# Transposes in halves, and another order of all instructions, in a long-convolution and MLP kernel

## The chip, the cores and the metric

The kernel runs on one core of one Trainium2 chip. The metric is the device time of one launch in microseconds (us), lower is better. A core has a matrix engine (TensorE, PE in the profile), VectorE (DVE), ScalarE (ACT), GpSimd (POOL) and SyncE (SP), each with an instruction list of its own that it works off strictly in order; 16 DMA engines move data for the queues of SP and POOL. Engines meet through semaphores: an instruction whose operand isn't ready waits, and everything behind it on its engine waits too.

## What is computed

One gated layer with two branches on 2048 rows of 640 columns, all in bf16:

```python
def _A_ref(q, k, v, shift_k, ssm_k, ssm_D):          # long convolution
    k_pad = jnp.pad(k, ((0, 0), (ks - 1, 0), (0, 0)))
    for t in range(ks):                              # ks = 4 taps along the rows
        k_shift = k_shift + k_pad[:, t:t + S, :] * shift_k[:, ks - 1 - t]
    kv = k_shift * v
    y = irfft(rfft(kv, 2 * S) * rfft(ssm_k, 2 * S))[:S]   # each column by itself
    return q * (y + kv * ssm_D)
def _B_ref(x, w1, w2, w3, w4):                       # MLP
    h = _gelu(_layernorm(x) @ w1)
    # the four quarters of h are moved by 1, -1, 2, -2 rows
    x1 = x + shifted(h) @ w2
    return x1 + _gelu(_layernorm(x1) @ w3) @ w4
g = _sigmoid((A_q * gate_w).sum(-1))
return g * _A_ref(A_q, ...) + (1 - g) * _B_ref(A_q, ...)
```

The column counts are 640 for the branches' inputs and outputs and 1536 for the inner width of the second MLP (w3, w4).

## The kernel before

**Recording, then emitting.** Small helpers (`tt` and `ts` for VectorE, `act` for ScalarE, `mm` for TensorE, `P.dma` for the queues) don't issue anything: each records an operation with what it reads and writes, in the order of the code. There are 1196 operations. `Prog.schedule` (line 255) then puts them into the order of one list, `SEQUENCE` (line 457), whose entries are indices of recording; `Prog.emit` (276) gives each engine its own operations in that order and adds the waits that the data needs. A second list, `PLACES` (522), gives each of the 205 accumulation tiles its bank of PSUM; an operation that opens a tile waits until the users of the bank's former tile are through. So the order of every engine, of SyncE's and POOL's DMA queues too, is one list written out by hand. As the helpers issue everything, the profile names their lines: L616 a VectorE operation on two tensors, L621 one with scalars, L626 ScalarE, L636 TensorE, L235 a transposing DMA, L238 any other DMA, L900 the residual of mm2.

**The convolution.** The 640 columns are five chunks c of 128, the 2048 rows four blocks of 512; the convolution is done block by block with a folded Fourier transform written as matrix products. A chunk passes these stages:
- `h_load` (712) loads 128 rows of the filter; `h_fold` (715) makes the sums and differences that a real transform of half the size needs, the four sums first (`sd[:, 0]`) and then the four differences (`sd[:, 1]`), and one DMA transposes all 2048 columns so that `h_chunk` (745) can take the spectrum HF on TensorE.
- `kv_load` (750) brings a chunk of keys and one of values from HBM through a transposing DMA each (2048 rows by 128 columns, 512 KB). Keys go to one of two buffers in turn (`kT[c % 2]`). `kv_taps` (757) makes the four shifted multiples of the keys on VectorE (four 2048-wide operations of L621, "taps"), adds them and multiplies by the values.
- `kv_fold` (777) is the same fold for that product, again with one transposing DMA at its end, and `x_chunk` (789) takes the spectrum XF. Chunks 1 to 4 use the same memory (`kv_at`, 559): the first tap of chunk c + 1 writes where the transpose of kv_fold-c reads, and its third tap where that transpose writes and x_chunk-c reads.
- `combine` (949) adds neighbouring blocks of XF. `unit` (955) multiplies spectra (2560-wide products of L616, and accumulating DMAs on POOL's queue for part of the sums). The buffers of the last units lie over those of the late folds.
- `final` (994) takes a unit back by matrix products with G, multiplies by q and adds to the output: the first 12 by an accumulating DMA on POOL's queue, whose VectorE buffer `gyb[k % 8]` is used again eight steps later, the last four by a plain write from SyncE.

**The MLP** works by row tiles t (16 of 128 rows) and row groups (four of 512). `ln1` (833) normalizes (the first half of the tiles is transposed on TensorE, the later ones by DMA), `mm1` (851) and `mmg` do the first product and the shifts, `mm2` (886) the second with the residual, `ln2` (906) normalizes again: its *apply* (L621, 640 wide) writes one of two buffers `xn2[t % 2]`, and a transposing DMA of 160 KB takes it into `xT`. So the apply of ln2-3 waits until the transpose of ln2-1 has read its buffer. `mm3` (917) and `mm4` (938) are the second MLP, `base` (933) writes the first part of the output rows, mm4 adds to it by an accumulating DMA on POOL's queue.

**SyncE's list** starts with 22 plain loads, then all transposes and later loads follow. In operations by name ("T" for a transpose, "k" and "v" for the keys and values of kv_load):

```
x_load-0 (2), x_load-1, x_load-0 (2), x_load-1, w1 (2), h_load-1, w2, h_load-0, x_load-3, x_load-2,
cR, w3 part 0, w2 (2), x_load-2, w2 (2), x_load-3, cRh,
kv_load-1 k T, kv_load-1 v T, kv_load-0 v T, h_fold-0 T, kv_load-0 k T, ln1-8 T, ln1-9 T, h_fold-1 T, ...
kv_load-4 k T, base-4, kv_load-3 v T, kv_fold-2 T, ln2-9 T, base-8, base-9, cG, ln2-8 T, w4, kv_load-4 v T, ...
```

cR and cRh are the constants of the forward transforms, w1 to w4 the weights.

Of the kernel before, what the change touches and what calls it, by code (L numbers as in the profile page):

```python
# [420 lines left out]
def bass_gated_mix__ssm_conv_h3__mixer_s_mlp__prompt_kernel(  # L421
# [4 lines left out]
    P = Prog(nc)  # L426
# [26 lines left out]
    def ps(n, cls):  # L453
# [3 lines left out]
    SEQUENCE = [27, 10, 47, 6, 0, 11, 29, 4, 9, 1, 3, 46, 2, 30, 5, 12, 8, 7, 26, 13, 131, 14, 49, 15, 48, 16, 28, 54, 17, 132,  # L457
# [257 lines left out]
    def h_fold(c):  # L715
# [11 lines left out]
        tt(sd[:, 1], pm[:, :, :, 0:128], rev, ALU.subtract)  # L727
        tt(sd[:, 0, 0, :, 0], pm[:, 0, :, 128], rev[:, 0, :, 0], ALU.add)
        ts(sd[:, 0, 1, :, 0], pm[:, 1, :, 128], 1.0, None, ALU.mult)
        P.dma(sp, ft, V(h_at[c], 2048), transpose=True)  # L730

    def spectrum(c, f, F_, even, odd):
        for j in range(4):
# [402 lines left out]
```

## Time and profile before

| | us |
|---|---|
| median of the runs (three) | 246.19 |
| lowest and highest of them | 245.36 and 246.31 |
| the profiled execution | 244.31 |
| its span, from the first to the last instruction | 242.5 |
| TensorE busy in the span | 217.8 (90%) |
| VectorE busy | 218.5 (90%) |
| ScalarE busy | 171.2 (71%) |
| POOL busy | 66.5 (27%) |

The profile is one execution, seen by the hardware profiler. An engine's busy time is the time of its instructions; the rest of the span it waits, for another engine or for a DMA, or for its own queue. Rows of the timeline give the start in us from the span's start, the length, the engine, the line, the operation with what it writes and reads, the count, and in brackets the idle time of the engine just ahead of it with what ended it. `arena` is the one large buffer in which nearly all data lie, so the names of buffers say little; which stage an instruction belongs to follows from its place in its engine's list. In a row of the groups, the time behind the bar is the busy time and the mean of one in ns, then the idle time ahead with its releasers. The queue's own rows (SPq) give what an issue occupied on SyncE.

### The profile page before, as it was taken

Reading aid. Unit: us, or ns where it says so; the run is one execution under the profiler, and the core shown is the slowest. Engines: PE = TensorE matmul, PEld = TensorE weight load, DVE = VectorE, ACT = ScalarE, POOL = GpSimd, SP = SyncE. Lnnn points to the kernel's source line nnn. Section 1 sums busy time; section 2 is a strip of 40 time slices with the busy share of each in tenths; the row PEclk is TensorE's granted clock in tenths of the full one; section 3 lists DMA queues with packets and bytes.
Section 4 is the critical chain, followed back from the end, with each engine's and each line's share of the span. In section 5 each row is a group of like instructions: output and inputs, shape, how many; then the busy total and the mean of one; then the engine's idle time right before and its main releaser. Section 6 shows DMA issues by size and latency. Waiting matters only on the chain.

```text
span 242.5 us, 3885 instructions
## 1 busy us (share of the span) xinstructions
PE 217.8 (90%) x1428; PEld 126.5 (52%) x1428; DVE 218.5 (90%) x431; ACT 171.2 (71%) x307; POOL 66.5 (27%) x70
## 2 busy tenths in 40 slices
PE   7889899898899987998889989999999999998950
PEld 2677675354344445345465437764576545775520
DVE  5999999999599868899599699999999999999974
ACT  2598569995689959997799766256876455246951
POOL 1311135402000011103342401431115203557591
PEclk9999999999999999999999999999999999999985
DMA  6999999999999998998918955399998914999998
GB/s 185 341 381 330 155 209 171 224 230 190 225 197 204 247 121 182 224 329 185 172 32 164 186 90 162 32 150 200 187 255 132 164 22 73 175 172 172 119 111 160
DMA packets 79970, 44.02 MB, mean 182 GB/s; under 512 B 59337, under 2 KB 75214, under 8 KB 79950
## 3 DMA queue, kind: packets, MB, share of 16 engines
q1 hardware_dynamic: 70944, 31.89, 56.1%
q0 software_dynamic: 8832, 11.80, 33.3%
q8 instruction: 11, 0.18, 0.3%
q10 hardware_dynamic: 174, 0.07, 0.1%
q14 instruction: 9, 0.07, 0.1%
HBM read 14.92 MB, written 6.55 MB: 89 GB/s over the span
## 4 chain that ended last, share of the span: by engine, by line
DVE 56%; DMA 20%; ACT 9%; issue 6%; PE 4%; POOL 2%; SPq 2%; POOLq 0%; DVEq 0%
DVE arena L616 45%; DMA arena<-arena 13%; ACT arena L626 9%; DVE arena L621 6%; PE PSall L636 4%; DMA out_dram<-arena 4%; DMA arena<-in_A_ssm_k_dram 3%; DVE arena L798 3%; DVE arena L865 2%; SPq L238 2%; POOL out_dram L238 1%; POOL arena L238 0%; DVE arena L799 0%; DVE arena L900 0%; DVE arena L682 0%
## 5 line engine op out<-in xcount | busy, mean ns | idle before, releaser
L636 PE MATMUL PSall<-arena 128*128 128x320 bf16 (+4 forms) x1367 | 209.4, 310 | 17.5 <-ACT arena L626 6.6
L636 PEld LDWEIGHTS PSall<-arena 128*128 128x128 bf16 x1367 | 122.0, 98 | 104.1 <-ACT arena L626 17.2
L616 DVE TENSOR_TENSOR arena<-arena 128x2560 bf16<-128x2560 bf16 (+9 forms) x217 | 162.6, 807 | 6.0 <-DMA arena<-arena 2.5
L626 ACT ACTIVATE arena<-PSall 128x512 bf16<-128x512 f32 (+7 forms) x169 | 102.3, 652 | 30.0 <-PE PSall L636 24.8
L626 ACT ACTIVATE arena<-arena 128x640 bf16<-128x640 bf16 (+6 forms) x72 | 49.1, 705 | 15.7 <-DVE arena L616 11.3
L802 POOL TENSOR_TENSOR arena<-arena 128x1 f32<-128x1 f32 (+1 forms) x26 | 23.1, 919 | 98.6 <-DVE arena L621 98.6
L621 DVE TENSOR_SCALAR arena<-arena 128x1 f32<-128x1 f32 (+5 forms) x110 | 33.5, 339 | 10.6 <-DMA arena<-arena 5.8
L238 POOL DMA_DIRECT2D out_dram<-arena x28 | 29.4, 1320 | 44.6 <-ACT arena L626 39.1
L626 ACT ACTIVATE arena<-PSall,arena 128x640 bf16<-128x640 f32 (+1 forms) x32 | 20.7, 653 | 18.9 <-PE PSall L636 18.8
L238 POOL DMA_DIRECT2D arena<-arena x12 | 14.5, 1205 | 27.4 <-DVE arena L616 25.2
L798 DVE BATCH_NORM_STATS2 arena<-arena 128x6 f32<-128x320 bf16 x32 | 14.3, 481 | 1.7 <-DMA arena<-in_A_q_dram 1.6
L662 PE MATMUL PSall<-arena 128*128 128x512 bf16 x15 | 5.8, 570 | 1.6 <-DVE arena L658 1.6
L900 DVE SCALAR_TENSOR_TENSOR arena<-PSall,arena 128x640 bf16<-128x640 f32 x8 | 6.5, 817 | 0.7 <-PE PSall L636 0.7
L865 DVE TENSOR_SCALAR arena<-arena 32x256 bf16<-32x256 bf16 (+1 forms) x24 | 5.8, 242 | 0.4
L626 ACT ACTIVATE PSall<-PSall 128x640 f32<-128x640 f32 x8 | 5.5, 692 | 0.1
L662 PEld LDWEIGHTS PSall<-arena 128*128 128x128 bf16 x15 | 2.0, 139 | 4.9 <-issue 3.0
L844 PE MATMUL PSall<-arena 128*128 128x128 bf16 x40 | 3.5, 220 | 0.6 <-DVE arena L621 0.5
L844 PEld LDWEIGHTS PSall<-arena 128*128 128x128 bf16 x40 | 2.4, 98 | 1.3 <-DVE arena L621 1.1
L665 ACT ACT_TABLE_LOAD x1 | 1.3, 1283 | 2.1 <-issue 2.1
L799 DVE BATCH_NORM_AGGREGATE arena<-arena 128x2 f32<-128x12 f32 x16 | 2.6, 190 | 0.0
L626 ACT ACTIVATION_READ_ACCUMULATOR arena<-arena 128x1 f32 x8 | 1.8, 221 | 0.0
L626 ACT ACTIVATION_READ_ACCUMULATOR arena<-PSall 128x1 f32 x8 | 1.6, 194 | 0.0
(21 smaller groups left out, 5.6 us busy)
## 6 DMA issues: line engine op xcount, KB each, us to landing
arena<-arena POOLq DMA_DIRECT2D x12, 640.0 KB, 6.7
arena<-in_A_q_dram SPq DMA_DIRECT2D x14, 320.0 KB, 6.2
out_dram<-arena POOLq DMA_DIRECT2D x20, 160.0 KB, 5.4
arena<-in_A_ssm_k_dram SPq DMA_DIRECT2D x5, 512.0 KB, 4.5
arena<-in_B_w_dram SPq DMA_DIRECT2D x1, 1920.0 KB, 9.1
out_dram<-arena SPq DMA_DIRECT2D x10, 160.0 KB, 2.3
arena<-in_B_w_dram SPq DMA_DIRECT2D x1, 1152.0 KB, 11.9
out_dram<-arena SPq DMA_DIRECT2D x12, 80.0 KB, 3.0
```

Of the source, the lines that this page charges most:

```text
L238: fn = lambda e: e.dma_start(out, in_, **kw)
L616: P.op(eng, lambda e: e.tensor_tensor(o, real(a), real(b), op), [a, b], [o], dve_ns(o, [a, b], 2) if eng == "dve" else 500)
L621: P.op(eng, lambda e: e.tensor_scalar(o, real(a), s1, s2, op0=op0, **({} if op1 is None else {"op1": op1})), [a] + aps, [o], n_of(o) / 3.8 ...
L626: P.op("act", lambda e: e.activation(real(o), real(a), f, bias=bias, scale=scale, **({"accum_out": accum} if accum is not None else {})), ...
L636: fns.append(lambda e, l=l, r=r, i=i: e.matmul(real(o), l, r, start=(i == 0), stop=(i == last)))
L662: P.op("pe", lambda e: e.matmul(real(pw), warm[:, 0:128], warm[:, 128:640], start=True, stop=True), [warm], [pw], 427.0 if i < 14 else 216.0)
L798: P.op("dve", lambda e, o=o, i=i: e.bn_stats(o, i), [i], [o], 400)
L799: P.op("dve", lambda e: e.bn_aggr(bna[:, t, :], bns[k]), [bns[k]], [bna[:, t, :]], 120)
L802: P.op("pool", lambda g: g.tensor_tensor(o, a, e, ALU.pow), [a, e], [o], dur)
L844: P.op("pe", [lambda e, c=c, pb=pb, xn=xn: e.transpose(real(pb)[:, 128 * c:128 * (c + 1)], xn[:, 128 * c:128 * (c + 1)], ident) for c in r ...
L865: P.op("dve", lambda e, o=hT[q, 4, c0:c0 + n], i=hx[q, :]: e.tensor_scalar(o, i, 1.0, None, op0=ALU.mult), [hx[q, :]], [hT[q, 4, c0:c0 + n ...
L900: P.op("dve", lambda e: e.scalar_tensor_tensor(x, real(pr), 1.0, x, op0=ALU.mult, op1=ALU.add, accum_out=st[1, 0][:, t:t + 1]), [pr, x], [ ...
```

## The change

The transposes of `h_fold`, `kv_load` and `kv_fold` (20 in all) are issued as two each: for keys and values the first and the second 1024 rows, for the folds the sums and the differences. Every other operation is recorded as before.

```diff
@@ h_fold
-        P.dma(sp, ft, V(h_at[c], 2048), transpose=True)
+        for i in range(2):
+            P.dma(sp, ft[:, 8 * i:8 * i + 8, :], V(h_at[c] + 1024 * i, 1024), transpose=True)
@@ kv_load
-        P.dma(sp, kT[c % 2][:, 16:2064].unsqueeze(1), A_k[0, :, cs], transpose=True)
-        P.dma(sp, V(kv_at[c], 2048).unsqueeze(1), A_v[0, :, cs], transpose=True)
+        for i in range(2):
+            P.dma(sp, kT[c % 2][:, 16 + 1024 * i:1040 + 1024 * i].unsqueeze(1), A_k[0, 1024 * i:1024 * i + 1024, cs], transpose=True)
+        for i in range(2):
+            P.dma(sp, V(kv_at[c] + 1024 * i, 1024).unsqueeze(1), A_v[0, 1024 * i:1024 * i + 1024, cs], transpose=True)
@@ kv_fold
-        P.dma(sp, V(kv_at[c] + 6144, 2048).rearrange("p (q c) -> p q c", q=16), V(kv_at[c] + 2048, 2048), transpose=True)
+        for i in range(2):
+            P.dma(sp, V(kv_at[c] + 6144 + 1024 * i, 1024).rearrange("p (q c) -> p q c", q=8), V(kv_at[c] + 2048 + 1024 * i, 1024), transpose=True)
```

`SEQUENCE` and `PLACES` are replaced as a whole (1216 operations, again 205 tiles):

```diff
-    SEQUENCE = [27, 10, 47, 6, 0, 11, 29, 4, 9, 1, 3, 46, 2, 30, 5, 12, 8, 7, 26, 13, 131, 14, 49, 15, 48, 16, 28, 54, 17, 132,
...
+    SEQUENCE = [27, 10, 46, 8, 1, 30, 11, 5, 9, 4, 0, 48, 3, 29, 2, 12, 28, 13, 47, 26, 14, 33, 15, 49, 16, 50, 17, 34, 51, 41,
...
-    PLACES = [0, 0, 2, 3, 1, 3, 7, 4, 1, 6, 7, 0, 4, 4, 2, 4, 2, 4, 0, 3, 2, 7, 0, 4, 1, 5, 7, 6, 2, 6, 7, 2, 1, 4, 4, 1, 0,
...
+    PLACES = [7, 2, 6, 0, 4, 2, 2, 3, 6, 6, 5, 6, 4, 2, 6, 0, 2, 5, 0, 5, 4, 5, 3, 0, 1, 7, 3, 1, 1, 0, 7, 1, 0, 7, 3, 1, 2,
...
```

By name, the places of the new order that matter below (a and b are the first and second half of a transpose):

```
SyncE, start: x_load-0 (3), w1, x_load-0, w1, x_load-1 (2), x_load-2, w2, h_load-0, w2 (4), x_load-2, x_load-3 (2),
  kv_load-1 k b, kv_load-0 k a, kv_load-0 k b, h_load-1, cRh, h_fold-0 a, h_fold-0 b, kv_load-0 v b, kv_load-1 k a,
  ln1-8 T, ln1-9 T, h_load-2, ...; w3 part 0 behind h_fold-2 a, cR behind kv_fold-1 a
SyncE, around ln2-3: kv_fold-0 b, a, ln2-0 T, ln2-1 T, kv_fold-1 b, h_fold-4 b, a, kv_fold-1 a, cR, ln2-3 T, ln2-2 T
SyncE, around kv_fold-2: kv_load-4 k b, kv_load-3 v b, ln2-7 T, kv_load-3 v a, kv_fold-2 b, a, ln2-6 T, w4, base-1, ln2-9 T
VectorE, from the last fold result to the buffer's next use:
  kv_fold-2 to kv_taps-3   before: three residuals of mm2, a tap, small ones; after: a tap, an apply of ln2, small ones
  kv_fold-3 to kv_taps-4   before: a tap, a combine, small ones; after: four combines, a tap, small ones
  kv_fold-4 to unit-0-3    before: two products, a small one; after: two products, a combine, small ones
TensorE, behind the start of x_chunk-2: before 7 groups of mm3-0 after its end; after 3, the others ahead of it
POOL, end, before: mm4-13, final-0-3-0, -0-1-0, -0-2-1, mm4-14, final-0-0-1, -0-0-0, -0-3-1, -0-1-1, final-1-...
POOL, end, after: mm4-15, mm4-14, final-0-1-1, -0-0-1, mm4-13, final-0-3-0, -0-2-0, -0-1-0, -0-3-1, -0-0-0, final-1-...
```

139 rows, old and new, of tables (PLACES, SEQUENCE) are left out of this document.

## The prediction

> **What bounds the kernel now.** The stretches come first: busy time of each engine, then granted clock, DMA share and GB/s.
>
> ```profile
> core 0: us, PE busy (x) PEld busy (x) DVE busy (x) ACT busy (x) POOL busy (x), PEclk, DMA share, GB/s
> 0.00:15.00 15.00, 11.99 (x121) 7.44 (x121) 11.80 (x49) 7.36 (x21) 3.28 (x9) 1.00 0.87 285
> 15.00:60.00 45.00, 40.21 (x338) 26.07 (x337) 43.96 (x133) 35.76 (x76) 10.83 (x12) 1.00 1.09 228
> 60.00:140.00 80.00, 73.61 (x397) 37.30 (x395) 65.81 (x129) 69.76 (x112) 14.87 (x15) 1.00 0.90 190
> 140.00:222.00 82.00, 81.06 (x512) 49.53 (x509) 81.73 (x82) 46.15 (x77) 25.82 (x26) 1.00 0.77 141
> 222.00:239.20 17.20, 10.98 (x67) 6.13 (x66) 15.20 (x44) 12.13 (x25) 11.69 (x10) 0.88 1.08 130
> ```
>
> From 140 to 222 TensorE (81.06 of 82) and VectorE (81.73 of 82) are both full, so nothing can be won there. VectorE is idle for 14.2 us between 60 and 140 and for 1.0 us between 15 and 60; TensorE is idle for 6.4 and 4.8 us there. The change removes no arithmetic. The run therefore gets shorter only by idle time that **both** engines lose before 140, or in the tail. Who ends that idle time is read from the waits between 60 and 140 (total, times, longest), then from single rows of the timeline.
>
> ```profile
> DVE arena L621 <- DMA arena<-arena: 5.3, 3, 2.8
> DVE arena L621 <- ACT arena L626: 3.9, 4, 2.8
> DVE arena L616 <- DMA arena<-arena: 2.2, 1, 2.2
> ACT arena L626 <- DMA arena<-arena: 4.0, 2, 2.5
> ```
>
> ```profile
> 65.56 0.45 DVE L621 TENSOR_SCALAR arena<-arena 128x640 bf16<-128x640 bf16 x1 [2.76 <-DMA arena<-arena]
> 90.59 0.74 ACT L626 ACTIVATE arena<-arena 128x640 bf16<-128x640 bf16 x1 [2.52 <-DMA arena<-arena]
> 91.45 0.21 DVE L621 TENSOR_SCALAR arena<-arena 128x1 f32<-128x1 f32 x1 [2.77 <-ACT arena L626]
> 117.67 0.75 DVE L621 TENSOR_SCALAR arena<-arena 128x2048 bf16<-128x2048 bf16 x1 [1.79 <-DMA arena<-arena]
> 120.09 0.74 ACT L626 ACTIVATE arena<-arena 128x640 bf16<-128x640 bf16 x1 [1.45 <-DMA arena<-arena]
> 135.31 1.49 DVE L616 TENSOR_TENSOR arena<-arena 128x2560 bf16<-128x2560 bf16 x1 [2.24 <-DMA arena<-arena]
> ```
>
> The reader is to see that every DMA named here goes from the arena to the arena on SyncE's queue: a transpose. By their place in VectorE's list the stalls are: 65.56, the apply of ln2-3, whose buffer xn2 the transpose of ln2-1 still reads; 91.45, ln2-8, behind the ScalarE square of mm2-8, which waits for the transpose of ln2-6; 117.67, the first tap of chunk 4, whose buffer the transpose of kv_fold-3 still reads; 135.31, the first product of unit-0-3 that goes into a buffer under kv_fold-4. The third wait of the first row (5.3 - 2.76 - 1.79, so 0.77) is the same for kv_fold-2 and chunk 3. TensorE stalls on the same thing:
>
> ```profile
> 44.42 12.55 PE L636 MATMUL PSall<-arena 128*128 128x512 bf16 x83 [1.06 <-DMA arena<-arena]
> 58.09 2.58 PE L636 MATMUL PSall<-arena 128*128 128x1 bf16 x20 [1.12 <-DMA arena<-arena]
> 61.67 9.79 PE L636 MATMUL PSall<-arena 128*128 128x512 bf16 x48 [1.00 <-DMA arena<-arena]
> 92.44 17.63 PE L636 MATMUL PSall<-arena 128*128 128x320 bf16 x89 [2.31 <-ACT arena L626]
> 121.88 18.38 PE L636 MATMUL PSall<-arena 128*128 128x320 bf16 x102 [1.43 <-ACT arena L626]
> ```
>
> The last two follow the ScalarE stalls at 90.59 and 120.09, so all five are late transposes: 6.9 us. **Late transposes are the bound of the stretch before 140.** Why they are late, SyncE's queue and the landings tell:
>
> ```profile
> 17.08 9.04 SPq L235 DMA_TRANSPOSE arena<-in_A_k_dram  x1
> 31.66 2.42 SPq L235 DMA_TRANSPOSE arena<-arena  x1
> 60.90 1.28 SPq L235 DMA_TRANSPOSE arena<-arena  x1
> L235 SPq DMA_TRANSPOSE arena<-arena x34: 1199/1278/3608, 31.7 to 148.0; - x34
> L235 SPq DMA_TRANSPOSE arena<-in_A_k_dram x5: 2286/3050/9036, 17.1 to 87.5; - x5
> L235 SPq DMA_TRANSPOSE arena<-in_A_v_dram x5: 1428/2133/2710, 26.2 to 108.3; - x5
> arena<-in_A_v_dram SPq DMA_TRANSPOSE x1, 4.1
> arena<-arena SPq DMA_TRANSPOSE x1, 2.6
> ```
>
> Rows of line 235 give issue time on SyncE (least, median, most, in ns); the last two are the landings of kv_load-4's value transpose at 108.35 (512 KB, 4.1 us) and of ln2-14's at 147.99 (160 KB, 2.6 us), both with little beside them. The first transpose holds SyncE until 26.1, while the plain loads before it drain.
>
> **The change, part by part.** *SyncE's start.* The old list puts 7.3 MB of plain loads ahead of the first transpose, the new one some 2.5 MB less (the 1152 KB of w3, 512 KB of h_load-1, cR's 384 and cRh's 480 KB go behind). At the 285 GB/s of the first row that is 9.1 us by which the first transposes can start earlier; h_fold-0's, issued at 31.66, stands in the new list directly behind what VectorE needs to make it. Nobody needs the loads that move back at once: w3 and cR are first used in stages after 75 us. h_load-1 and cRh are needed earlier, by VectorE's h_fold-1 and TensorE's h_chunk-0 near 25 to 30 us; both now stand behind three key halves on SyncE, at 1.2 to 2.13 us each 3.6 to 6.4 us, less than the 9.1 won. If that cover is gone, each us that they are late costs one us of both engines there. *Halves.* A 160 KB transpose takes 1.2 us of SyncE at the least, a 512 KB one 1.4 to 3.6, so two halves cost 2.4 against a middle of 2.6 (medians 2.13 and 3.05). The trace has no 256 KB transpose; between the rows above it lands in 2.6 + 1.5 x 96/352 = 3.0 us. From 1.2 us a half (2.4 a pair) to 2.13 (4.3 a pair), I take 1.3, nearest to the many small ones: 12 pairs stand before ln2-2 in the new list, and cost nothing as long as the lead of 9.1 us covers them. I charge 0.5 us for what shows.
>
> *VectorE's order around the folds.* For this I count the work that stands between the last instruction that feeds a transpose and the first that needs its buffer, at busy time over count of these groups:
>
> ```profile
> L616 DVE TENSOR_TENSOR arena<-arena 128x2560 bf16<-128x2560 bf16 x52 | 74.7, 1480 | 2.3 <-DMA arena<-arena 2.2
> L616 DVE TENSOR_TENSOR arena<-arena 128x1024 bf16<-128x1024 bf16 x40 | 26.1, 683 | 0.2
> L616 DVE TENSOR_TENSOR arena<-arena 128x1280 bf16<-128x1280 bf16 x28 | 22.2, 814 | 0.3 <-DMA arena<-arena 0.3
> L621 DVE TENSOR_SCALAR arena<-arena 128x2048 bf16<-128x2048 bf16 x20 | 14.8, 745 | 3.4 <-DMA arena<-arena 2.6 <-PE PSall L636 0.8
> L900 DVE SCALAR_TENSOR_TENSOR arena<-PSall,arena 128x640 bf16<-128x640 f32 x8 | 6.5, 817 | 0.7 <-PE PSall L636 0.7
> L636 PE MATMUL PSall<-arena 128*128 128x512 bf16 x430 | 97.1, 379 | 3.3 <-DMA arena<-arena 2.1 <-ACT arena L626 0.5 <-DVE arena L621 0.3
> ```
>
> That is 1.44 us for a unit product, 0.65 for a fold half, 0.79 for a combine, 0.74 for a tap, 0.82 for a mm2 residual; the smallest I take at 0.15.
> - kv_fold-4 to unit-0-3: before 2 products and a small one, 3.0; after 2 products, a combine and four small, 4.3. The stall of 2.24 shrinks by 1.3, and by up to 0.65 more because the first half leaves after one fold subtraction or sum and not after both. I take -1.9 (from -1.3 to -2.2).
> - kv_fold-3 to chunk 4: before a tap, a combine and three small, 2.0; after four combines, a tap and three small, 4.4. All of the 1.79 goes: -1.8.
> - kv_fold-2 to chunk 3: before three residuals, a tap and six small, 4.1; after a tap, one 640-wide apply and four small, 1.8. **This one gets worse by 2.3.** Its half b is queued first and waits for the later of the two fold results, so the split wins nothing here. Behind this tap in VectorE's list stand all taps of chunk 3, and ln2-9 and ln2-8.
> - ln2-3: about as much work between (6.8 after, 6.4 before), but ln2-1's transpose now stands behind kv_fold-0's and not behind a key transpose of 512 KB; ln2-6: its transpose is now queued behind both halves of kv_fold-2. Each wins between 0 and 2.77; the trace can't say more, I take half: -1.4 each.
>
> Sum for VectorE: -1.9 - 1.8 + 2.3 - 1.4 - 1.4 = -4.2.
>
> *TensorE's order.* It must win as much. In the old list h_chunk-2 follows h_fold-2 so closely that TensorE has 3.8 us more work ahead of it than VectorE has ahead of the fold; in the new one this is over 6 for every transpose that TensorE uses, against 4.1 to 5 us for issue and landing. I count two thirds of the 6.9 us as gone, 4.6, which covers VectorE's 4.2. One wait is added: the third tap of chunk 3 overwrites what x_chunk-2 reads, and in the new list four more groups of mm3-0 (20 matmuls at 0.226, 4.5 us) stand before the end of x_chunk-2; with 0.7 less VectorE work before the tap the wait tightens by 5.2. 2.3 of it are the kv_fold-2 stall already counted, the other 2.9 are covered if TensorE has won 2.9 by then; four of its five stalls (5.5 us) lie before that place, two thirds are 3.7. So nothing, and 2.9 if not. *PSUM banks*: new places alter who waits for whose eviction; TensorE's waits for ScalarE beside the two above are small, so 0, within 1 us either way.
>
> *Tail.* POOL's last accumulating writes free VectorE's gy buffers:
>
> ```profile
> 229.51 6.17 POOL L238 DMA_DIRECT2D out_dram<-arena  x5 [2.35 <-DVE arena L616]
> 233.39 3.62 DVE L616 TENSOR_TENSOR arena<-arena 128x320 bf16<-128x320 bf16 x14 [1.55 <-DMA out_dram<-arena]
> ```
>
> The write of final-0-3-1-1 moves ahead of two others on POOL's queue, but VectorE has 5.2 instead of 6.1 us of work until it reuses that buffer: 0, from -1.6 to +1.
>
> **Sum:** -4.2 + 0.5 = -3.7 us. The profiled execution (span 242.5) took 244.31 us, 1.9 less than the median of the three runs, 246.19. 244.31 - 3.7 = 240.6; the same difference from the median gives 242.5.
>
> The Trainium skill, "DMA: Bandwidth & Descriptors", section "Rules for kernel authors", speaks against the split: two transfers to disjoint halves use the same 16 engines and serialize, so one should be used. The landings of 4.1 and 2.6 us agree with a part that doesn't scale. By that rule the 0.65 us of the early half go, and the sum is about -3.1: 243.1.
>
> **Rivals.** *Forecast*, 240 to 245: chance 0.52. *More*: all five TensorE stalls go, and VectorE's waits at best (-2.2, -1.8, -2.8, -2.8, tail -1.6, +2.3 for kv_fold-2, so -8.9) are capped by TensorE's 6.9: 239.3. For it speaks that both engines are full afterwards; against it, that the chain from kv_fold-2 gets longer, and that TensorE's ScalarE waits at 92.44 and 121.88 go only if both ln2 transposes come earlier. 0.16. *Traded*: TensorE doesn't get ahead, and the 2.9 us at x_chunk-2 stand: -3.7 + 2.9 = -0.8, 245.4. For it speaks that DMA is at 1.09 between 15 and 60 whatever the order. 0.14. *Slower*: the queue. Place: SyncE, from the first transpose to ln2-2. If a half takes as long as what a whole value transpose takes in backlog, the 24 halves push everything behind them. It decides from (9.1/12 + 2.6)/2 = 1.7 us a half, where the lead is used up; at 1.9 it is 24 x 0.19 = 4.6 us late on both engines: 250.8. For it: SyncE issues without a pause from 17 to 75; against it: the median of 1.28. 0.18. The same section's rule to coalesce small transfers would favour this case.
>
> **Numbers.** 0.5% of 246.19 is 1.2 us, about what a measurement can tell from no change. Forecast and *more* are faster, 0.68; *traded* is the same, 0.14; *slower* 0.18. The range leaves out the lower end of *more* and the upper of *slower*: 237.5 to 248.5; the forecast's own is 240 to 245.
>
> **What would show it.** Right: the first transpose issued before 17 and finished before 20; VectorE idle under 10.5 between 60 and 140; the waits at chunk 4 and unit-0-3 under 0.7 each, that at chunk 3 near 3; TensorE's waits for DMA arena<-arena under 1.1. Wrong: a median issue of halves above 1.7 us, VectorE waiting over 4 us for TensorE at chunk 3, or a tail after TensorE's full stretch longer than 17 us.

## The result, and the profile after

| | us |
|---|---|
| kernel before, median of 20 runs | 245.9 (243.41 to 247.66) |
| changed kernel, median of 20 runs | 247.55 (245.83 to 250.44) |
| ratio, 95% interval | 1.008 (1.0051 to 1.0109) |
| profiled execution of the changed kernel, its span | 246.26, 244.5 |

The change makes the kernel 0.8% slower, where 1.5% faster was forecast: about 2 us lost instead of 3.7 won. The ratio leaves out the slowest executions (one of the changed kernel, two of the one before), so it is not quite that of the two medians. The stretches of the changed kernel, in the columns of before:

```profile
core 0: us, PE busy (x) PEld busy (x) DVE busy (x) ACT busy (x) POOL busy (x), PEclk, DMA share, GB/s
0.00:15.00 15.00, 12.72 (x150) 8.70 (x151) 11.99 (x49) 7.99 (x23) 3.55 (x9) 1.00 0.91 285
15.00:60.00 45.00, 40.90 (x301) 25.03 (x303) 43.46 (x117) 35.97 (x76) 6.00 (x6) 1.00 1.05 204
60.00:140.00 80.00, 71.76 (x406) 37.49 (x412) 68.37 (x142) 62.49 (x99) 16.60 (x16) 1.00 0.89 180
140.00:222.00 82.00, 75.14 (x465) 46.19 (x468) 75.09 (x77) 48.17 (x83) 37.77 (x28) 0.96 0.84 160
222.00:244.00 22.00, 15.01 (x100) 8.90 (x97) 19.29 (x49) 13.87 (x27) 14.66 (x13) 0.92 1.10 139
```

From 60 to 140 VectorE is idle for 11.6 us instead of 14.2: something was won there. But from 140 to 222, where both engines had been full, each is now idle for 6.9 us. What they wait for, from the waits of that stretch (total, times, longest):

```profile
PE PSall L637 <- ACT arena L627: 6.6, 1, 6.6
DVE arena L617 <- DMA arena<-arena: 6.0, 1, 6.0
```

It is one event. (The changed kernel's lines stand one to five further down than those of before: L617 is its L616, L622 its L621, L807 the power on POOL that was L802. The kernels of experiments 3, 5, 8, 9 and 10 have the line numbers of before.) The chain that ended last, in order of time, runs through it; the columns are start, length and what:

```profile
153.70 0.14 DVE arena L622
153.84 0.07 issue
153.91 10.19 POOL arena L807
164.09 7.56 DMA arena<-arena
171.75 3.64 DVE arena L617 x3
```

By their places in the lists: at 153.70 VectorE makes the variance of ln2-14. POOL raises it to the power -1/2, an operation on 128x1 elements that for the other tiles of ln2 took between 0.5 us (0.55 for ln2-11) and 2.5 us (2.46 for ln2-13) in this execution and lasts 10.2 us here. Behind it on POOL's queue stands the second accumulating DMA of unit-0-2, whose last operand VectorE had finished at about 156. It is issued at 164.09 and lands at 171.66. VectorE needs the sum and stops for 6.02 us; ScalarE's next copy waits for VectorE and TensorE for ScalarE. During the power VectorE runs eight two-tensor operations back to back, and the power ends 0.4 us after the last of them:

```profile
153.74 9.97 DVE L617 TENSOR_TENSOR arena<-arena 128x1280 bf16<-128x1280 bf16 x8
153.91 10.22 POOL L807 TENSOR_TENSOR arena<-arena 128x1 f32<-128x1 f32 x1 [0.58 <-DVE arena L622]
```

In the kernel before, the power of ln2-14 ran at 134.0, in VectorE's wait for kv_fold-4, and took 1.05 us:

```profile
134.00 1.05 POOL L802 TENSOR_TENSOR arena<-arena 128x1 f32<-128x1 f32 x1
```

TensorE's stop is followed by a lower granted clock, 0.57 between 172 and 180, which is the 0.96 of the stretch; VectorE is busy without a pause there, so no further loss is seen from it.

The waits of VectorE between 60 and 140, from the waits and the timeline:

```profile
DVE arena L622 <- DMA arena<-arena: 6.6, 3, 4.6
DVE arena L617 <- issue: 1.9, 1, 1.9
```

```profile
88.34 1.23 DVE L617 TENSOR_TENSOR arena<-arena 128x2048 bf16<-128x2048 bf16 x1 [1.86 <-issue]
90.49 0.45 DVE L622 TENSOR_SCALAR arena<-arena 128x640 bf16<-128x640 bf16 x1 [0.93 <-DMA arena<-arena]
100.55 0.75 DVE L622 TENSOR_SCALAR arena<-arena 128x2048 bf16<-128x2048 bf16 x1 [4.58 <-DMA arena<-arena]
116.70 0.75 DVE L622 TENSOR_SCALAR arena<-arena 128x2048 bf16<-128x2048 bf16 x1 [1.05 <-DMA arena<-arena]
```

Gone are the waits at ln2-3 (2.76), ln2-8 (2.77), unit-0-3 (2.24) and in the tail (1.55). The tap behind kv_fold-2 waits 4.58 instead of 0.77, that behind kv_fold-3 1.05 instead of 1.79. New are 1.86 at chunk 2's product with its values (their second half landed at 88.26) and 0.93 at ln2-7. Together -9.32 + 3.81 - 0.74 + 1.86 + 0.93 = -3.46 us. With the 6.02 us behind POOL that is +2.6, and the spans differ by +2.0; the rest are small waits and 0.3 us less busy time.

SyncE's issues say why kv_fold-2 got worse by more than the 2.3 foreseen:

```profile
89.02 2.64 SPq L235 DMA_TRANSPOSE arena<-in_A_k_dram  x2
91.71 1.28 SPq L235 DMA_TRANSPOSE arena<-in_A_v_dram  x1
93.04 1.27 SPq L235 DMA_TRANSPOSE arena<-arena  x1
94.36 1.30 SPq L235 DMA_TRANSPOSE arena<-in_A_v_dram  x1
95.70 4.35 SPq L235 DMA_TRANSPOSE arena<-arena  x3
L235 SPq DMA_TRANSPOSE arena<-in_A_k_dram x10: 1287/1300/4510, 10.1 to 107.4; - x10
L235 SPq DMA_TRANSPOSE arena<-in_A_v_dram x10: 1233/1300/1333, 27.3 to 115.6; - x10
arena<-arena SPq DMA_TRANSPOSE x3, 3.5
```

The fold was done at about 94.6. Its two halves were issued at 95.70 and 97.05, behind four halves of keys and values and a transpose of ln2, each 1.3 us on SyncE. A half takes as long to issue as the short ones of before and lands in 3.5 us (the last row, the median of the two halves and the 160 KB transpose that follows), where 3.0 was estimated.

### The profile page after: what moved, and what is told of

Same layout as the page of the kernel before. It is cut to its first block, busy times and chain, and to the rows that moved or that the text cites. A ratio compares the mean times of both kernels' runs of the same rounds, so it can differ in the third digit from the quotient of the medians.

```text
span 244.5 us, 3915 instructions
## 1 busy us (share of the span) xinstructions
PE 215.5 (88%) x1413; PEld 126.3 (52%) x1428; DVE 218.2 (89%) x431; ACT 168.5 (69%) x307; POOL 78.6 (32%) x70
## 4 chain that ended last, share of the span: by engine, by line
DVE 38%; PE 21%; DMA 19%; POOL 7%; SPq 5%; issue 5%; ACT 2%; DVEq 0%; POOLq 0%
DVE arena L617 26%; PE PSall L637 21%; DMA arena<-arena 11%; DVE arena L622 6%; POOL arena L807 5%; SPq L235 5%; DVE arena L803 4%; DMA arena<-in_A_v_dram 3%; POOL out_dram L238 2%; DMA arena<-in_A_ssm_k_dram 2%; DMA out_dram<-arena 2%; DMA arena<-in_A_q_dram 2%; ACT arena L627 2%; DVE arena L870 1%; SPq L238 1%
## 5 line engine op out<-in xcount | busy, mean ns | idle before, releaser
L637 PE MATMUL PSall<-arena 128*128 128x320 bf16 (+4 forms) x1352 | 208.3, 311 | 20.6 <-ACT arena L627 11.6
L617 DVE TENSOR_TENSOR arena<-arena 128x2560 bf16<-128x2560 bf16 (+7 forms) x217 | 163.6, 810 | 10.8 <-DMA arena<-arena 6.0
L627 ACT ACTIVATE arena<-PSall 128x512 bf16<-128x512 f32 (+6 forms) x169 | 100.8, 647 | 41.7 <-PE PSall L637 37.4
L807 POOL TENSOR_TENSOR arena<-arena 128x1 f32<-128x1 f32 (+1 forms) x26 | 35.1, 1374 | 108.6 <-DVE arena L622 108.5
L627 ACT ACTIVATE arena<-arena 128x640 bf16<-128x640 bf16 (+6 forms) x72 | 48.2, 697 | 17.5 <-DVE arena L617 14.3
L622 DVE TENSOR_SCALAR arena<-arena 128x1 f32<-128x1 f32 (+5 forms) x110 | 33.5, 339 | 7.1 <-DMA arena<-arena 6.7
L238 POOL DMA_DIRECT2D out_dram<-arena x28 | 32.0, 1492 | 12.3 <-ACT arena L627 10.6
L238 POOL DMA_DIRECT2D arena<-arena x12 | 16.7, 1434 | 39.3 <-DVE arena L617 39.3
L627 ACT ACTIVATE arena<-PSall,arena 128x640 bf16<-128x640 f32 (+1 forms) x32 | 20.1, 658 | 9.4 <-PE PSall L637 9.1
L627 ACT ACTIVATION_READ_ACCUMULATOR PSall<-PSall 128x1 f32 x8 | 1.6, 197 | 0.0
```

The lines of the kernel that those rows point to most:

```text
L238: fn = lambda e: e.dma_start(out, in_, **kw)
L617: P.op(eng, lambda e: e.tensor_tensor(o, real(a), real(b), op), [a, b], [o], dve_ns(o, [a, b], 2) if eng == "dve" else 500)
L622: P.op(eng, lambda e: e.tensor_scalar(o, real(a), s1, s2, op0=op0, **({} if op1 is None else {"op1": op1})), [a] + aps, [o], n_of(o) / 3.8 ...
L627: P.op("act", lambda e: e.activation(real(o), real(a), f, bias=bias, scale=scale, **({"accum_out": accum} if accum is not None else {})), ...
L637: fns.append(lambda e, l=l, r=r, i=i: e.matmul(real(o), l, r, start=(i == 0), stop=(i == last)))
L807: P.op("pool", lambda g: g.tensor_tensor(o, a, e, ALU.pow), [a, e], [o], dur)
```

## The experiments

Lists below name instructions in the order of one engine; everything else is as in the kernel named. Each ratio is to the kernel before on the same chip.

**1. The power behind the DMA.** Theory: the wait is a queue, and the power has no turn while VectorE is busy. On POOL, in the changed order:

```diff
-  mm4-5, power of ln2-14, unit-0-2 second DMA, mm4-4
+  mm4-5, unit-0-2 second DMA, power of ln2-14, mm4-4
```

> The changed kernel with one instruction moved: on POOL, the small operation of ln2-14 (L807, 128x1) stands behind the second accumulating DMA of unit-0-2, not ahead of it. In the changed kernel that operation lasted 10.22 us (153.91 to 164.13, while VectorE ran eight two-tensor products without a pause), the DMA behind it was issued at 164.09 though its data were ready at about 156, and VectorE waited 6.02 us for its landing at 171.66. Theory (the queue): the DMA is issued near 156, lands before 165, VectorE's wait of 6.02 is under 0.5, and the time falls by 5 to 6.5 us, to 241 to 242.5, below the kernel before. The POOL operation still lasts until VectorE pauses. Rival (slow DMA): the DMA lands late anyway, because POOL cannot issue while VectorE runs or because the 16 engines are taken; VectorE still waits 4 us or more there and the time is within 1 us of 247.5. Rival (elsewhere): the wait goes but another takes its place further on; 245 to 247.5.

Measured 241.15 us, ratio 0.9841 (0.9789 to 0.9893): by the ratios 2.4% or 5.9 us under the changed kernel, and faster than before. POOL's part of the timeline:

```profile
158.24 1.20 POOL L238 DMA_DIRECT2D arena<-arena  x1 [2.92 <-DVE arena L617]
158.98 7.14 POOL L807 TENSOR_TENSOR arena<-arena 128x1 f32<-128x1 f32 x1
```

The DMA is issued while VectorE is busy, in the usual 1.20 us, as soon as its operand is there (this execution ran 2 us later than the one above), and lands at 164.09, 3.5 us before VectorE needs it. The power still lasts 7.14 us, until VectorE pauses for its result. So the place behind the power in POOL's queue is what cost the time, and neither POOL's issuing nor the DMA engines.

**2. A pause for the power.** The rival to test is that the power is slow by itself. POOL's list is left as it is; on VectorE the instruction of ln2-14 that needs the power moves up:

```diff
-  unit-0-2 product 3, six operations, ln2-14 (waits for POOL)
+  unit-0-2 product 3, ln2-14 (waits for POOL), six operations
```

> The changed kernel with one instruction moved: on VectorE, the small operation of ln2-14 that waits for POOL's result stands directly behind the product that ends at 155.96 (unit-0-2, product 3) instead of six instructions later, so VectorE pauses there. POOL's list is that of the changed kernel. Theory (POOL's operation gets no turn while VectorE runs two-tensor operations back to back): it ends some 0.4 us after VectorE has paused, so it lasts 2.3 to 2.8 us instead of 10.2; VectorE waits about 0.5 us for it, the wait of 6.02 goes, the time is 241 to 243. Rival (the operation is slow by itself at this place, for instance because POOL has first to fetch something): it still lasts about 10 us, VectorE waits about 8 us for it, and the time is 246.5 or more.

Measured 240.3 us, ratio 0.9822 (0.9777 to 0.9866).

```profile
154.45 2.47 POOL L807 TENSOR_TENSOR arena<-arena 128x1 f32<-128x1 f32 x1 [0.58 <-DVE arena L622]
156.89 1.20 POOL L238 DMA_DIRECT2D arena<-arena  x1
156.96 0.16 DVE L617 TENSOR_TENSOR arena<-arena 128x1 f32<-128x1 f32 x1 [0.46 <-POOL arena L807]
```

VectorE gives up 0.46 us and the power takes 2.47 us instead of 10.22. The rival falls: what the power lacks is a turn.

**3. The new order with whole transposes.**

```diff
@@ kv_fold; h_fold and kv_load likewise, each at the place of its later half
-        for i in range(2):
-            P.dma(sp, V(kv_at[c] + 6144 + 1024 * i, 1024).rearrange("p (q c) -> p q c", q=8), V(kv_at[c] + 2048 + 1024 * i, 1024), transpose=True)
+        P.dma(sp, V(kv_at[c] + 6144, 2048).rearrange("p (q c) -> p q c", q=16), V(kv_at[c] + 2048, 2048), transpose=True)
```

> The new order of everything with whole transposes: each pair of halves is one transpose of 512 KB at the place of the later half. It tells what the halves are worth in the new order. By the prediction's step they cost 0.5 us of queue and win 0.65 us at unit-0-3, so nothing: 246.5 to 248.5, with the same 6 us wait behind POOL. Rival (halves burden SyncE's queue or the DMA engines): the time falls by 2 us or more, below 245.5. Rival (halves are what the new order rests on): over 249.5, with waits of VectorE for transposes in the stretch from 60 to 140 grown by 2 us or more.

Measured 246.59 us, ratio 1.004 (1.0004 to 1.0076). The wait behind POOL is there as before:

```profile
152.58 10.22 POOL L802 TENSOR_TENSOR arena<-arena 128x1 f32<-128x1 f32 x1 [0.58 <-DVE arena L621]
170.43 1.49 DVE L616 TENSOR_TENSOR arena<-arena 128x2560 bf16<-128x2560 bf16 x1 [6.04 <-DMA arena<-arena]
```

Against the changed kernel's 1.008 the halves would cost about 1 us, but the two intervals overlap, so this alone does not show it. Both rivals fall: the time is neither 2 us lower nor 3 us higher.

**4. The old order with halves**, the two of a pair directly behind each other.

> The old order of everything, with each of the 20 whole transposes issued as two halves directly behind each other. It tells the price of the halves alone. By the prediction's row (2.4 us for a pair against a middle of 2.1 for a whole) the queue before 60 us grows by some 4 us for 12 pairs and, without the earlier start, part of it shows: 246.5 to 249.5. Rival (a half costs as much as a whole on the queue): over 250. Rival (the early half wins everywhere): under 245.

Measured 248.83 us, ratio 1.0141 (1.0085 to 1.0198): 3.5 us for the halves alone where the order wasn't made for them. So they are not free there; what the new order is worth without them, the next experiment tells.

**5. Whole transposes and the pause**, experiments 2 and 3 together.

> The new order with whole transposes, and the VectorE instruction of ln2-14 that waits for POOL moved up to directly behind unit-0-2's product 3, so that VectorE pauses for it. Theory (two independent costs: the wait behind POOL, about 6 us, and the halves, about 1 us): that POOL operation lasts 2.3 to 2.8 us, the wait of 6.04 is gone, and the time is 6 us under that of the new order with whole transposes (246.6) and some 1 us under the same edit with halves (240.3): 238.5 to 240.5. Rival (the halves' early part pays once the large wait is gone): over 241.

Measured 238.72 us, ratio 0.9758 (0.9706 to 0.981), as the sum of the two costs would have it. Beside experiment 2 the halves cost 0.64% or 1.6 us; here too the intervals overlap, but both comparisons point the same way. The new order alone, without halves and without the wait behind POOL, is worth 2.4% or 5.9 us.

**6. Halves for the folds alone.** Experiment 2 with the transposes of keys and values whole:

```diff
@@ kv_load
-        for i in range(2):
-            P.dma(sp, kT[c % 2][:, 16 + 1024 * i:1040 + 1024 * i].unsqueeze(1), A_k[0, 1024 * i:1024 * i + 1024, cs], transpose=True)
-        for i in range(2):
-            P.dma(sp, V(kv_at[c] + 1024 * i, 1024).unsqueeze(1), A_v[0, 1024 * i:1024 * i + 1024, cs], transpose=True)
+        P.dma(sp, kT[c % 2][:, 16:2064].unsqueeze(1), A_k[0, :, cs], transpose=True)
+        P.dma(sp, V(kv_at[c], 2048).unsqueeze(1), A_v[0, :, cs], transpose=True)
```

> The new order with the same VectorE instruction moved up as before, the transposes of h_fold and kv_fold in halves and those of keys and values whole. It tells which halves cost. Theory (an issue takes about 1.3 us on SyncE whatever its size, so every extra one costs the same, where the queue is full): between the run with all halves (240.3) and that with none (expected 238.5 to 240.5), and VectorE's wait for the transpose of kv_fold-2 shrinks from 4.8 to about 3.5, as the value halves before it are gone. Rival (the folds' halves pay by leaving early): at or below the run with none, with a wait under 2.5 there.

Measured 236.38 us, ratio 0.9661 (0.9606 to 0.9715): the fastest of all, 3.4% under the kernel before. The halves of keys and values cost 1.6% or 3.9 us beside experiment 2, and there the intervals do not touch. The theory, that every extra issue costs the same, would have put the time between experiment 5 and experiment 2 and falls: the folds' halves do not cost, they seem to win (experiment 5, on the same chip, has 238.72; the two intervals just touch, so the win itself is not shown). The tap behind kv_fold-2 in experiment 2, here, and in experiment 5:

```profile
100.72 0.75 DVE L622 TENSOR_SCALAR arena<-arena 128x2048 bf16<-128x2048 bf16 x1 [4.81 <-DMA arena<-arena]
```

```profile
96.95 0.75 DVE L622 TENSOR_SCALAR arena<-arena 128x2048 bf16<-128x2048 bf16 x1 [3.82 <-DMA arena<-arena]
```

```profile
96.91 0.75 DVE L621 TENSOR_SCALAR arena<-arena 128x2048 bf16<-128x2048 bf16 x1 [3.07 <-DMA arena<-arena]
```

At this tap halves of any kind cost, the folds' 0.75 us and the others' 1.0. If the folds' halves win, it is elsewhere; one place where less is lost are TensorE's waits for transposes, first in experiment 5, then here:

```profile
PE PSall L636 <- DMA arena<-arena: 5.5, 3, 2.4
```

```profile
PE PSall L637 <- DMA arena<-arena: 3.8, 3, 2.0
```

**7. Mending the tap behind kv_fold-2.** Experiment 6 with that fold's transpose whole and ahead of a value transpose on SyncE:

```diff
-  ln2-7 T, kv_load-3 v T, kv_fold-2 b, a, ln2-6 T
+  ln2-7 T, kv_fold-2 T, kv_load-3 v T, ln2-6 T
```

> The fastest so far (halves for the folds alone, VectorE pausing for ln2-14's power; 236.4) with two edits at the wait that the changed order made longer: the transpose of kv_fold-2 is whole again, and it stands ahead of the value transpose of kv_load-3 on SyncE. Before them SyncE issued that value transpose until 92.16 though the fold was done at 91.71, and the second half landed at 96.92, 3.82 us after VectorE had nothing else to do. Theory (issue on SyncE is the price, some 1.3 us for every transpose): issued near 91.8, landed near 96.1, the wait is 2.7 to 3.2 and the time 0.5 to 1.2 us less, 235.2 to 236.2. Rival (the wait moves to the product with chunk 3's values, or to TensorE): within 0.4 us of 236.4 or more.

Measured 238.57 us, ratio 0.978 (0.9714 to 0.9846): no gain, and on another chip than experiment 6 it is rather slower. Nine of the ten folds' transposes are still in halves here, and the ratio is that of experiment 5 (0.9758), one more reason not to count on their win. The wait shrank from 3.82 to 3.26, near the theory, but two others appeared right behind:

```profile
96.36 0.75 DVE L622 TENSOR_SCALAR arena<-arena 128x2048 bf16<-128x2048 bf16 x1 [3.26 <-DMA arena<-arena]
100.11 0.21 DVE L622 TENSOR_SCALAR arena<-arena 128x1 f32<-128x1 f32 x1 [0.94 <-ACT arena L627]
109.10 0.69 DVE L617 TENSOR_TENSOR arena<-arena 128x1024 bf16<-128x1024 bf16 x1 [1.97 <-ACT arena L627]
```

Where SyncE has no slack, a transpose pulled ahead pushes the next back; ln2-6's was issued at 96.23 instead of 94.93 and landed at 99.16, and the ScalarE operation that the first of the two new waits (0.94) is for started at 99.24, when a transpose had landed. Where the second (1.97) comes from was not traced.

**8. A useless power in the kernel before.** If POOL had to wait for VectorE's next pause in every case, one small operation should break the old order too:

```diff
+    pool_pow(st[0, 3][:, 0:1], st[0, 3][:, 1:2], neghalf[:, 0:1])
-  POOL: mm4-7, unit-0-2 first DMA
+  POOL: mm4-7, the power above, unit-0-2 first DMA
```

> The kernel before with one small operation more, a 128x1 power on POOL (L802) whose result nobody reads, put on POOL's list between the write of mm4-7 and the first accumulating DMA of unit-0-2. In the kernel before VectorE runs without a pause from 146 to 179.7 there. Theory (POOL's operation gets no turn until VectorE pauses, and the DMA behind it is late): it starts near 154.5 and lasts until VectorE waits for that DMA, near 171.5, so about 17 us; the DMA is issued at 171.5 to 172 instead of 155.8 and lands 6 us later, VectorE waits 6 to 7 us there, and the time rises by 5.5 to 8 us. Rival (the operation in the changed kernel was slow for another reason of its place): it lasts 0.5 to 2.5 us and the time rises by less than 1 us.

Measured 244.29 us, ratio 0.9999 (0.9967 to 1.0031), so this expectation of mine fell:

```profile
149.52 9.23 DVE L616 TENSOR_TENSOR arena<-arena 128x2560 bf16<-128x2560 bf16 x7
153.60 2.01 POOL L802 TENSOR_TENSOR arena<-arena 128x1 f32<-128x1 f32 x1
```

The power ended 0.4 us after the end of the second product that overlapped it (155.21), in the middle of an unbroken row of products. So POOL can be let in between two operations; the rule "not before VectorE pauses" is too strong.

**9. Trains of one kind.** Behind the end of the kernel before, rows of like VectorE operations, here called trains, with a power on POOL that can start behind the second of each (in one train the third). From the second of the two kernels, with fifteen trains:

```diff
+    train(1, [BT(BO[i], 2560) for i in range(8)])          # 128x2560, each output elsewhere
+    train(2, [BT(BO[i % 3], 2560) for i in range(8)])      # outputs in rotation
+    train(3, [BT(BO[i % 3], 1024, op=ALU.add) for i in range(12)])
+    train(4, [BT(BO[i % 8] + 1280 * (i // 8), 1024, op=ALU.add) for i in range(12)])
...
```

The first kernel has five kinds:

> The kernel before with five trains of VectorE operations added behind its end, in each a 128x1 power on POOL that can start behind the train's second operation. The trains: 8 two-tensor products 128x2560 bf16 with operands that don't depend on each other; 16 one-tensor operations with a scalar, 128x2048 bf16; 20 statistics 128x320; 12 two-tensor sums 128x1024; 8 two-tensor products of 128x2560 each of which needs the one before. Theory (two-tensor operations that follow without a pause leave POOL no turn): the power lasts to the end of the train in the first and fourth (about 9 and 7 us), about 0.55 us in the third, and in the fifth it gets its turn in the pauses between dependent products, so 1 to 2.5 us; for the second (one tensor, no earlier row with many in a run) either 0.55 to 1.5 us or to the train's end, about 10 us. Rival (any busy VectorE blocks POOL): to the train's end in all five. Rival (none does): under 2.5 us in all five.

The power took 1.74 us among products of 2560, 1.28 among one-tensor operations, 0.55 among statistics (as when nothing else runs), 6.35, to the train's end, among sums of 1024, and 1.79 among dependent products. That refuted both a block by any busy VectorE and the theory as stated, and led to fifteen trains that differ in one thing at a time:

> The kernel before with fifteen trains of two-tensor VectorE operations behind its end, a 128x1 power on POOL able to start behind the second or third of each. They differ in one thing at a time: 2560 wide with every operation's output elsewhere (1) and with outputs in rotation, so that each carries a wait for an earlier one (2); the same for 1024 (4 and 3); 1280 (5), strided 1280 between products of 2560 as in the late units (6), strided 1280 alone (7); two powers in a row (8 for 2560, 15 for 1024); the power one operation later (9); 2048, 1536, alternating 2560 and 1024, 640, 320 (10 to 14). In the earlier run the power lasted 1.74 us in a train of 2560 and to the train's end, 6.35 us, in one of 1024. Theory (whether the next operation already waits behind the one that runs): short ones (up to 2.5 us) where operations carry a wait, to the end where they carry none, so 2 short, 1 long. Rival (width): 1, 2, 8, 9 all short and 3, 4, 15 all long, with a border between 1024 and 2560 in 5, 10 and 11. Rival (the moment at which it starts within an operation): no such order, and the two powers of 8 and 15 differ.

POOL's rows for trains 1 to 4:

```profile
243.97 1.74 POOL L802 TENSOR_TENSOR arena<-arena 128x1 f32<-128x1 f32 x1 [4.80 <-DVE arena L621]
255.29 8.74 POOL L802 TENSOR_TENSOR arena<-arena 128x1 f32<-128x1 f32 x1 [9.58 <-DVE arena L621]
265.56 0.93 POOL L802 TENSOR_TENSOR arena<-arena 128x1 f32<-128x1 f32 x1 [1.53 <-DVE arena L621]
272.90 6.35 POOL L802 TENSOR_TENSOR arena<-arena 128x1 f32<-128x1 f32 x1 [6.42 <-DVE arena L621]
```

Train 2 has the form that gave 1.74 in the first kernel and gives 8.74 here; train 3 has the one that gave 6.35 and gives 0.93. So neither width nor waits decide. Nor does the place of the data: trains 2 and 8 are the same operations on the same buffers, and the power took 8.74 us in 2 and 1.73 in 8, where a second one stands behind it. Nor does the moment at which the power starts, 0.16 us into an operation in every train. In each train the power is let in at the end of an early operation or not before the train's last one: long in trains 2, 4, 7, 9, 11 and 14. The same kernel once more:

> The kernel of the run before with fifteen trains, once more, unchanged. In that run the power lasted to the train's end in trains 2, 4, 7, 9, 11 and 14 and at most 1.8 us in the others, in no order by width or by waits. Theory (the fine timing of the program decides, and it is the same in every execution): the same six trains are long. Rival (chance in every execution): other trains are long, the number near six.

```profile
242.50 1.74 POOL L802 TENSOR_TENSOR arena<-arena 128x1 f32<-128x1 f32 x1 [4.76 <-DVE arena L621]
253.82 8.74 POOL L802 TENSOR_TENSOR arena<-arena 128x1 f32<-128x1 f32 x1 [9.59 <-DVE arena L621]
264.09 0.93 POOL L802 TENSOR_TENSOR arena<-arena 128x1 f32<-128x1 f32 x1 [1.53 <-DVE arena L621]
271.43 6.35 POOL L802 TENSOR_TENSOR arena<-arena 128x1 f32<-128x1 f32 x1 [6.42 <-DVE arena L621]
```

The same six trains are long. So where VectorE's own operation starts the power, it is not chance from execution to execution: it repeats, in the two executions profiled. What decides is not shown. That fits the changed kernel: 10.22 us in its profile and again in experiment 3, and no run of 20 near 241. The same instruction can still go either way from one kernel to another: the power of ln2-15, at the same place of POOL's list, took 2.33 us in the changed kernel and in experiment 3, and 8.0 us in experiments 1, 2, 5, 6 and 7, where VectorE lost no more than 0.5 us to it.

**10. Twelve useless powers in the kernel before**, behind twelve of POOL's DMAs.

> The kernel before with twelve 128x1 powers on POOL whose results nobody reads, one behind each of twelve of its DMAs between 150 and 191 us, where VectorE runs without a pause. A single one, behind mm4-7, had lasted 2.01 us and cost nothing. Theory (POOL is let in at the boundary of two VectorE operations only where VectorE's next one isn't yet waiting behind the one that runs; so it depends on the place): some of the twelve last 0.5 to 2.5 us, others 4 to 10 us to the next pause; where one of the long kind stands ahead of an accumulating DMA of a unit, VectorE waits for that DMA, and the time rises by 2 to 8 us. Rival (the single place in the changed order is peculiar, for another reason): all twelve under 2.6 us and the time within 1 us of the kernel before. Rival (chance at each boundary): the time scatters over 2 us or more between runs of this same kernel.

Ten executions fall into two groups, five of 242.8 to 244.34 us and five of 254.7 to 258.49; the ratio, 0.9985 (0.9942 to 1.0027), is of the first group alone. In the profiled execution, of the first group (243.5 us), all twelve took 2.2 us or less, as the rival of a peculiar place has it. But the same kernel scatters by 12 us between its executions, which is the sign of the rival of chance; the power's start isn't tied to VectorE's operations here. Long powers may have made the second group, but no execution of it was profiled, so this is not shown.

## Why the prediction was wrong

**The bound.** Right before 140 for VectorE: late transposes ended its waits, and 9.3 us of them and of the tail went. Wrong behind it: "both full, so nothing can be won there" was read as "nothing happens there". That is the step that failed. A full stretch can't win, but it can lose, and the sum had no term for POOL's list in that stretch. The power of ln2-14 was moved from a wait of VectorE into a row of products, and ahead of a DMA that VectorE needs. Both could be seen in the lists. The wait that came in its place is 6.02 us of VectorE. Without that one wait the new kernel comes out at -3.8 us (experiment 1, 241.15 beside 244.97; -4.7 in experiment 2), next to the forecast -3.7. That nearness is partly luck, as the terms below show: some that were not foreseen cancel.

**SyncE's start.** Right:

```profile
10.08 10.18 SPq L235 DMA_TRANSPOSE arena<-in_A_k_dram  x3
23.57 1.77 SPq L235 DMA_TRANSPOSE arena<-arena  x1
```

The first transpose was issued at 10.08 instead of 17.08, h_fold-0's at 23.57 instead of 31.66: 8.1 us earlier, 9.1 estimated. But the three key halves ahead of h_load-1 and cRh held SyncE for 10.2 us, where 3.6 to 6.4 were reckoned and 9.1 was the cover. It cost nothing that shows: between 15 and 60 VectorE has no wait above 0.6 us, and TensorE is idle for 4.1 us, before 4.8.

**Halves.** The issue was sized right (1.3 us in the median), the effect too small: 0.5 us charged, 1.0 to 1.6 in the new order (not clear of noise), 3.5 in the old one. The prediction's cover, the lead of 9.1 us, didn't reach to 90 us, where SyncE is full again. The rule that the prediction takes from the Trainium skill, "DMA: Bandwidth & Descriptors", section "Rules for kernel authors" (one transfer, not two), is given there for halves by partitions; these are halves along the columns, each over all 128 partitions. Carried over to them, it pointed the right way for keys and values; for the folds, where the first half has a use of its own, experiments 5 and 6 rather speak against it, experiment 7 does not.

**VectorE around the folds.** kv_fold-4: -1.9 forecast, -2.24 came. kv_fold-3: -1.8 forecast, -0.74 came, because the halves' issue held the transpose up. kv_fold-2: +2.3 forecast, +3.8 came, for the same reason: with whole transposes (experiment 3) the two taps wait 0.37 and 2.93 us, which is -1.4 and +2.2. ln2-3 and ln2-8: half of each counted, all of both came. These five make -4.7 (-2.24 - 0.74 + 3.81 - 2.76 - 2.77), where -4.2 was forecast. New waits at chunk 2's values and ln2-7, 2.8 us, were not foreseen, and the tail, put at 0, won 1.55: -3.5 in all.

**TensorE.** Its waits for transposes did not fall by two thirds. Of the five counted, the three direct ones are 3.2 us in the whole run before, and there are six of 3.8 after; for the two that came through ScalarE, ScalarE's own waits for transposes between 60 and 140 fell from 4.0 to 1.2 us. In all TensorE is idle for 12.3 us between 15 and 140, before 11.2. It is 12.3 in experiment 2 too, which is 4.7 us faster than the kernel before. So the prediction's condition that the run gets shorter only by idle time that both engines lose before 140 or in the tail is not borne out for TensorE before 140. The other wait that was feared, for x_chunk-2 at the third tap of chunk 3, did not come.

**Rivals.** None of them had the mechanism. The slower one named the queue of SyncE; the halves did fill it, yet a median of 1.30 us is far from its 1.7, and the time was lost on POOL's queue.

## What to carry to other kernels

Walk every queue through a stretch that is full, not only through those that wait: name for each instruction that is moved what stands behind it on its engine, and what it needs from an engine that never pauses. A tiny POOL operation that reads SBUF is a risk ahead of a DMA that the path needs while VectorE runs two-tensor operations in a row: 6.0 us here, nothing in experiment 8. Put it behind, or give it a pause, which cost 0.46 us here and won six. Split a transpose only where somebody uses the first half early: the folds in halves with whole keys and values, in the new order with the pause, make the fastest kernel of this study, 236.38 us, though its lead over whole transposes (238.72) is not clear of noise.

## What was not expected of the hardware

A POOL operation on 128x1 elements, 0.55 us when alone, lasted up to 10.2 us beside a row of two-tensor VectorE operations, and in other cases of the same form was let in after one of them. The Trainium skill, "SBUF — State Buffer", section "Who interferes with whom", has the ground: a VectorE instruction with two inputs in SBUF and a GpSimd one that reads SBUF share an interface, and the one that comes second is blocked until the first is through. The runs agree that two-tensor operations block and that statistics do not (0.55 us in their train). They differ in how long: in the changed kernel seven operations that began after the power went ahead of it, and the same form gave 1.74 or 8.74 us. Which of the two it is repeats from execution to execution where VectorE starts the power; what in the timing decides it stays open. The DMAs that POOL issues were not held up by the products: 1.20 us with VectorE busy throughout.
